# Attention outputs with the tile index innermost, turned and sent in later slots; other slots for the last attention steps; the residual in four double loads

## The chip, the core and the metric

The kernel runs on one core of one Trainium2 chip. The core has five engines that run side by side, each in its own program order, tied together by semaphores: PE (TensorE, matrix products), DVE (VectorE), ACT (ScalarE), POOL (GpSimd) and SP (SyncE, which here issues all transfers, in one queue, in program order). The metric is the time of one execution on the device in microseconds (us). Three executions of the kernel before took 1117.1, 1117.71 and 1118.11 us, the median being 1117.71 us.

## What is computed

One transformer block with its two branches side by side, for 2048 tokens of width 576, all in fp32:

```python
def _A_ref(x, wqkv, wo):             # H = 32 heads of 18, W = 8 keys, distance 2
    q, k, v = split(x @ wqkv)
    idx = pos[:, None] - 2 * arange(8)[None, :]      # 8 earlier tokens, masked below 0
    logits = einsum("bhsd,bhswd->bhsw", q, k[idx]) * scale
    attn = softmax(logits)
    o = einsum("bhsw,bhswd->bhsd", attn, v[idx])
    return o @ wo
def _B_ref(x, w1, b1, w2):           # 576 -> 4608 -> 576
    h = x @ w1 + b1
    return mish(h) @ w2
xn = layernorm(x)
return x + _A_ref(xn, wqkv, wo) + _B_ref(xn, w1, b1, w2)
```

## The kernel before

**Tiling.** The tokens are worked through in two halves of 1024, called `hf` 0 and 1. In a half, token p * 8 + j sits on partition p in tile j, so j (0 to 7, `TJ` = 8) is the tile index. Each fp32 operand of a product is split into a high part and a rest, and each product is the sum of three.

**Dense branch.** The 4608 hidden columns are taken 256 at a time, in 18 steps called quads (q = 0 to 17). A quad of a half is six parts of the first product (`m1_part`, 0 to 5, with Mish on ACT behind each finished bank and a rest for the second product on POOL, L719). The second product of quad q runs among the parts of quad q + 1; from quad 8 of half 1 on it comes in four chunks of 24 matrix instructions each (`m2_cols`, L878). Each chunk fills four PSUM banks, which DVE adds to the accumulators (L881). Four banks are all that this product has, so PE can run at most one chunk ahead of DVE.

**Attention.** It runs on POOL and DVE under the matrix work. The 32 heads of a half are taken four at a time, as eight pairs of units, and a pair takes nine steps: four in which POOL multiplies queries by shifted keys (L538), one with the softmax, four in which POOL multiplies the weights by shifted values (L576). DVE's sum over the product of a step (L543 into `L`, L582 into `og`) is issued at the start of the next step. After the fourth value sum of a pair, `o_send` is called at once: DVE turns `og` in 32x32 blocks into `oT` (L597), and SP sends `oT` with four transfers (L601) to `o_d`, a scratch tensor in the chip's memory. `og` has the layout [partition, tile, column], so the turn reads it with the tile index innermost, at steps of 72 elements.

**Output product.** At the end, `wo_part(p, part)` for p = 0 to 7 (two token tiles each, L1064) multiplies the attention outputs by `wo`. The outputs are loaded back by `o_load` (L890 and L893, three transfers a tile, into a ring of five buffers), summed and split by `o_split` (ACT L912 to L942, DVE L915 to L940, POOL L941 and L943), and DVE adds each finished bank to the residual (L1068). For half 0 the residual, x plus the dense branch, was put into the scratch tensor `y_d`; `y_load(j)` (L1039) fetches it tile by tile into the four-buffer ring `raw`, so the load of tile 4 waits until tile 0 has been sent to the output (L1074).

**Order.** It is written out by hand. `plan` is a list of slots, each a piece of PE work. Work of other engines is hung on slots with `before(slot, fn)`. In each slot there is run, in this order: what was put on the list `soon` during the slot before, the slot's hung work, and then PE's own work. At the end every engine's instructions are tied in program order. Attention steps are laid on slots by a table of rates and by the list `ok`, which says which slots of a quad may take one: for quads of half 1 from 10 on, slots 0, 3, 5, 7 and 9 of ten (slots 0, 1, 3, 5, 7 and 9 are parts of the first product there, 2, 4, 6 and 8 chunks; in quad 17, slots 3, 5, 7 and 9 are chunks). The last two steps of half 1 fall on the first two slots of the output product.

Of the kernel before, what the change touches and what calls it, by code (L numbers as in the profile page):

```python
# [8 lines left out]
F32 = mybir.dt.float32  # L9
# [8 lines left out]
P = 128  # L18
# [4 lines left out]
TJ = SH // P  # L23
# [16 lines left out]
def block_kernel(ctx: ExitStack, tc: tile.TileContext, x, wq, wo, w1, b1, w2, mask, out):  # L40
# [470 lines left out]
    def attention(hf):  # L511
        kqs = [load_kq(hf, k) for k in range(PU)]
        yield
        behind = [None]

        def flush():
            if behind[0] is not None:
                behind[0]()
                behind[0] = None

        for pair in range(NQ * UQ // PU):
            n = f"{hf}_{pair}"
            vs, nxt = [], []
            L = sb.tile([P, PU, TJ, W, 2], F32, tag="L", bufs=2, name=f"L_{n}")
            hj = TJ // 2
            for k, (kt, q) in enumerate(kqs):
                for c in range(2):
                    flush()
                    pr = sb.tile([P, hj, W, CU], F32, tag="pr", bufs=2, name=f"pr_{n}_{k}_{c}")
                    j0 = c * hj  # L530
                    hh = hj // 2
                    on = hf and pair == 0
                    if on:
                        nc.vector.tensor_tensor(
                            out=pr, in0=q[:, j0:j0 + hj, None, :].to_broadcast([P, hj, W, CU]),
                            in1=win(kt, 0, CU, j0, hj), op=ALU.mult)
                    for x in () if on else range(0, hj, hh):
                        nc.gpsimd.tensor_tensor(  # L538
                            out=pr[:, x:x + hh], in0=q[:, j0 + x:j0 + x + hh, None, :].to_broadcast([P, hh, W, CU]),
                            in1=win(kt, 0, CU, j0 + x, hh), op=ALU.mult)  # L540

                    def red(pr=pr, k=k, j0=j0, L=L):
                        nc.vector.tensor_reduce(  # L543
                            L[:, k, j0:j0 + hj].rearrange("p j w h -> p (j w h)"),
                            pr.rearrange("p j w (h d) -> p (j w h) d", h=2), axis=AX, op=ALU.add)
                    behind[0] = red
                    if k == 0:
                        vs.append(load_kv(hf, pair * PU + c, 1))
                    yield
            flush()  # L550
            if hf == 0:
                lm = L[0:2].rearrange("p k j w h -> p k (j w h)")
                nc.vector.tensor_add(lm, lm, mk[:, None, :].to_broadcast([2, PU, TJ * W * 2]))
            m = sb.tile([P, PU * TJ, 2], F32, tag="m", bufs=2, name=f"m_{n}")
            Lf = L.rearrange("p k j w h -> p (k j) w h")
            Lt = Lf.rearrange("p j w h -> p j h w")
            nc.vector.tensor_reduce(m, Lt, axis=AX, op=ALU.max)
            mb = m[:, :, None, :].to_broadcast([P, PU * TJ, W, 2])
            nc.vector.tensor_sub(Lf, Lf, mb)
            Ls = L.rearrange("p k j w h -> p (k j w h)")  # L560
            if (hf, pair) == (0, 4):
                soon.append(lambda: nc.scalar.preload_act_table_set("natural_log_exp_and_others"))
            soon.append(lambda Ls=Ls: nc.scalar.activation(Ls, Ls, AF.Exp, scale=SCALE))
            if (hf, pair) == (0, 4):
                soon.append(root1)
            yield
            nc.vector.tensor_reduce(m, Lt, axis=AX, op=ALU.add)
            nc.vector.reciprocal(m, m)
            nc.vector.tensor_mul(Lf, Lf, mb)  # L569
            og = sb.tile([P, TJ, PU * CU], F32, tag="og", bufs=1, name=f"og_{n}")  # L570
            for k, vt in enumerate(vs):
                for h in range(2):
                    flush()
                    pr = sb.tile([P, TJ, DH, W], F32, tag="pr", bufs=2, name=f"pv_{n}_{k}_{h}")
                    for x in range(0, TJ, hj):
                        nc.gpsimd.tensor_tensor(  # L576
                            out=pr[:, x:x + hj].rearrange("p j d w -> p j w d"),
                            in0=L[:, k, x:x + hj, :, h:h + 1].to_broadcast([P, hj, W, DH]),
                            in1=win(vt, h * DH, DH, x, hj), op=ALU.mult)

                    def red(pr=pr, og=og, c0=k * CU + h * DH, last=(k, h) == (PU - 1, 1), pair=pair):
                        nc.vector.tensor_reduce(og[:, :, c0:c0 + DH], pr, axis=AX, op=ALU.add)  # L582
                        if last:
                            o_send(hf, pair, og)
                    behind[0] = red
                    if (hf, pair, k, h) == (0, *(4, 0, 1)):
                        newton1()
                    if k == 0 and (pair + 1) * PU + h < NQ * UQ:
                        nxt.append(load_kq(hf, (pair + 1) * PU + h))
                    yield  # L590
            kqs = nxt
        flush()
        yield

    def o_send(hf, pair, og):
        oT = sb.tile([P, PU * CU * TJ], F32, tag="oT", bufs=1, name=f"oT_{hf}_{pair}")
        nc.vector.transpose(oT.rearrange("p (c j) -> p c j", j=TJ), og.rearrange("p j c -> p c j"))  # L597
        rows = o_d[hf][pair * PU * CU:(pair + 1) * PU * CU].rearrange("(n c) j p -> (c j) n p", c=4)
        for g in range(4):
            part = slice(g * 32, (g + 1) * 32)  # L600
# [433 lines left out]

    ys = {}

    def y_load(j):
        ys[j] = sb.tile([P, 5 * P], F32, tag="raw", bufs=4, name=f"y_{j}")
        nc.sync.dma_start(ys[j][:, 0:D], y_d.rearrange("(p j) d -> p j d", j=TJ)[:, j, :])  # L1039

    def y_store(j):
        nc.sync.dma_start(y_d.rearrange("(p j) d -> p j d", j=TJ)[:, j, :], accs[0][j])
# [3 lines left out]
    def wo_part(p, part):  # L1046
        hf, j = divmod(2 * p, TJ)
        od = ops[p]
        A, B, S = od["A"], od["B"], od["S"]
        ts = [ys[j + k][:, 0:D] for k in range(2)] if hf == 0 else None  # L1050
        ov = out[hf * SH:(hf + 1) * SH, :].rearrange("(p j) d -> p j d", j=TJ)
        A11, A12 = A[:, :, 0:2], A[:, :, 2:4]
        A22 = B[:, 0:2]
# [288 lines left out]
    def spot(hf, q, i):  # L1342
        return at["s", hf, q, i]
# [137 lines left out]
    for hf in range(NH):  # L1481
        for q in range(1, NP):
            for i in range(10):
                ok[spot(hf, q, i)] = i in ((0, 3, 7, 9), (0, 3, 5, 7, 9))[hf] and (q > 1 or i)

    for q in range(2 * OC + 2):
        for i in range(spot(1, q, 0), spot(1, q, 9) + 1):
# [42 lines left out]
    for n, name in enumerate(("T1", "T4", "D", "B22")):  # L1530
        before(j + n // 2, lambda name=name: wo_fetch(name))
    for k in range(2):
        before(j + -1, lambda k=k: (o_load(0, k), y_load(k)))
        before(at["o", 0, 0], lambda k=k: (o_load(0, 2 + k), y_load(2 + k)))
    for k in range(4):
        before(j + (1, 1, 2, 3)[k], lambda k=k: o_split(0, k, True))
    for k in range(4, 2 * TJ):
        before(at["o", k // 2 - 2, 0], lambda k=k: o_load(*divmod(k, TJ)))
        if k < TJ:
            before(at["o", k // 2 - 1, 1], lambda k=k: y_load(k))  # L1540

    for i, (fns, bg, _) in enumerate(plan):
        first, soon[:] = soon[:], []
# [49 lines left out]
```

## Time and profile before

| what | value |
|---|---|
| median of three executions | 1117.71 us |
| the profiled execution's own time | 1116.71 us |
| its span | 1114.9 us |
| PE busy | 1100.3 us, 99% of the span |
| DVE, POOL, ACT busy | 76%, 70%, 45% |
| granted TensorE clock | full in every slice |
| moved by DMA | 271.08 MB, mean 243 GB/s |

The span is the time from the first to the last instruction in the profile; the time of the profiled execution is 1.8 us longer, which lies around the span. A row of the timeline gives the start and the duration of a run of equal instructions, the engine, the line, the tiles as written<-read, and in square brackets the idle time of the engine before it and what ended it. "issue" there stands for time in which the engine waited for nothing that the profile shows. A row of the windows gives, for a stretch of time, the busy time of each engine with the number of instructions, the granted clock, the share of the DMA engines and the rate.

### The profile page before, as it was taken

Reading aid. Unit: us, or ns where it says so; the run is one execution under the profiler, and the core shown is the slowest. Engines: PE = TensorE matmul, PEld = TensorE weight load, DVE = VectorE, ACT = ScalarE, POOL = GpSimd, SP = SyncE. Lnnn points to the kernel's source line nnn. Section 1 sums busy time; section 2 is a strip of 40 time slices with the busy share of each in tenths; the row PEclk is TensorE's granted clock in tenths of the full one; section 3 lists DMA queues with packets and bytes.
Section 4 is the critical chain, followed back from the end, with each engine's and each line's share of the span. In section 5 each row is a group of like instructions: output and inputs, shape, how many; then the busy total and the mean of one; then the engine's idle time right before and its main releaser. Section 6 shows DMA issues by size and latency. Waiting matters only on the chain.

```text
span 1114.9 us, 18235 instructions
## 1 busy us (share of the span) xinstructions
PE 1100.3 (99%) x6550; PEld 1013.6 (91%) x6550; DVE 852.4 (76%) x1371; ACT 497.9 (45%) x916; POOL 776.8 (70%) x631
## 2 busy tenths in 40 slices
PE   8999999999999999999999999999999999999998
PEld 7999899999999999999999889988999999999898
DVE  6369788888889888897666576686776677787886
ACT  5544645544554534555232355353442443433353
POOL 2479777766679687785787336666779878768732
PEclk9999999999999999999999999999999999999999
DMA  6899696868766849666697797664665466876664
GB/s 205 282 312 317 221 351 215 293 226 276 263 242 240 295 152 365 236 240 216 189 336 251 215 368 263 234 220 145 240 219 186 173 231 220 291 239 198 220 202 140
DMA packets 175134, 271.08 MB, mean 243 GB/s; under 512 B 49570, under 2 KB 116420, under 8 KB 175044
## 3 DMA queue, kind: packets, MB, share of 16 engines
q1 hardware_dynamic: 175044, 269.91, 70.9%
q8 instruction: 52, 0.85, 0.3%
q14 instruction: 38, 0.31, 0.1%
HBM read 160.39 MB, written 109.48 MB: 242 GB/s over the span
## 4 chain that ended last, share of the span: by engine, by line
PE 87%; DVE 4%; POOL 3%; DMA 2%; ACT 1%; issue 1%; SPq 1%; DVEq 0%; ACTq 0%; POOLq 0%
PE h L667 29%; PE po L765 21%; PE pq L348 9%; PE po L878 9%; PE po L857 7%; PE h L673 6%; PE o L1064 4%; PE z L446 3%; DMA o<-o_d 1%; POOL pv L576 1%; POOL s L618 1%; DVE og L582 1%; POOL accP L866 1%; DMA wo<-wkept_B 1%; POOL act L719 0%
## 5 line engine op out<-in xcount | busy, mean ns | idle before, releaser
L765 PEld LDWEIGHTS po<-w,act 128*128 128x128 f32 x1728 | 236.4, 188 | 6.0 <-POOL act L719 0.4
L765 PE MATMUL po<-w,act 128*128 128x288 f32 x1728 | 240.7, 295 | 0.1
L576 POOL TENSOR_TENSOR pv<-L,kv 128x576 f32<-128x576 f32 x128 | 175.9, 1472 | 38.1 <-DVE L L569 28.6
L719 POOL TENSOR_TENSOR act<-c,act 128x512 fp32r<-128x512 f32 x81 | 107.7, 1330 | 126.2 <-ACT act L718 125.5
L538 POOL TENSOR_TENSOR pr<-q,kv 128x576 f32<-128x576 f32 x120 | 184.2, 1560 | 6.4 <-DMA q<-q_d 4.6
L769 DVE TENSOR_TENSOR acc<-po,acc 128x288 f32<-128x288 f32 x288 | 119.5, 448 | 29.6 <-PE po L765 28.3
L348 PE MATMUL pq<-wq,xt 128*128 128x432 f32 x672 | 136.3, 361 | 1.0 <-ACT xt L81 0.6
L878 PEld LDWEIGHTS po<-w,act 128*128 128x128 f32 x960 | 131.1, 188 | 4.3 <-DVE accP L881 1.0
L878 PE MATMUL po<-w,act 128*128 128x288 f32 x960 | 133.9, 295 | 0.6 <-DVE accP L881 0.5
L348 PEld LDWEIGHTS pq<-wq,xt 128*128 128x128 f32 x672 | 125.1, 188 | 7.8 <-ACT xt L81 1.4
L713 ACT ACTIVATE c<-c,b1c 128x512 f32<-128x512 f32 x81 | 58.7, 725 | 135.1 <-DVE c L712 134.7
L667 PE MATMUL h<-xt,t 128*128 128x512 f32 x432 | 110.5, 391 | 0.7 <-DVE rt L712 0.7
L667 PE MATMUL h<-S,t 128*128 128x512 f32 x432 | 110.4, 391 | 0.0
L582 DVE TENSOR_REDUCE og<-pv 128x144 f32<-128x1152 f32 x64 | 85.9, 1343 | 26.9 <-POOL pv L576 26.7
L701 ACT COPY c<-h 128x512 f32<-128x512 f32 x81 | 47.5, 586 | 129.7 <-PE h L673 75.3
L667 PE MATMUL h<-xt,wa 128*128 128x512 f32 x432 | 104.1, 390 | 0.0
L543 DVE TENSOR_REDUCE L<-pr 128x64 f32<-128x1152 f32 x64 | 85.8, 1342 | 15.0 <-POOL pr L538 14.9
L667 PEld LDWEIGHTS h<-xt,wa 128*128 128x128 f32 x432 | 80.9, 188 | 17.0
L881 DVE TENSOR_TENSOR accP<-po,accP 128x288 f32<-128x288 f32 x160 | 69.5, 453 | 34.4 <-PE po L878 33.1
L857 PEld LDWEIGHTS po<-pw,u 128*128 128x128 f32 x672 | 92.1, 188 | 2.9 <-DVE u L811 0.7
L857 PE MATMUL po<-pw,u 128*128 128x288 f32 x672 | 93.7, 295 | 0.5 <-DVE u L811 0.5
L667 PEld LDWEIGHTS h<-xt,t 128*128 128x128 f32 x432 | 79.0, 188 | 15.7 <-DVE rt L712 1.2
(229 smaller groups left out, 1850.8 us busy)
## 6 DMA issues: line engine op xcount, KB each, us to landing
kv<-kv_d SPq DMA_DIRECT2D x64, 396.0 KB, 5.3
kept_t<-t SPq DMA_DIRECT2D x36, 512.0 KB, 5.3
t<-kept_t SPq DMA_DIRECT2D x36, 512.0 KB, 5.5
rw<-in_w SPq DMA_DIRECT2D x36, 320.0 KB, 4.5
kept_wa<-wa SPq DMA_DIRECT2D x18, 640.0 KB, 5.5
kept_w<-w SPq DMA_DIRECT2D x20, 576.0 KB, 5.2
wa<-kept_wa SPq DMA_DIRECT2D x18, 640.0 KB, 5.0
w<-kept_w SPq DMA_DIRECT2D x20, 576.0 KB, 4.2
```

Of the source, the lines that this page charges most:

```text
L348: nc.tensor.matmul(pq[:, 0:432], XT[:, xi, tok], wt[wi][:, hl, 0:432], start=i == 0, stop=i == len(seq) - 1)
L538: nc.gpsimd.tensor_tensor(out=pr[:, x:x + hh], in0=q[:, j0 + x:j0 + x + hh, None, :].to_broadcast([P, hh, W, CU]), in1=win(kt, 0, CU, j0 + ...
L543: nc.vector.tensor_reduce(L[:, k, j0:j0 + hj].rearrange("p j w h -> p (j w h)"), pr.rearrange("p j w (h d) -> p (j w h) d", h=2), axis=AX, ...
L576: nc.gpsimd.tensor_tensor(out=pr[:, x:x + hj].rearrange("p j d w -> p j w d"), in0=L[:, k, x:x + hj, :, h:h + 1].to_broadcast([P, hj, W, DH]),
L582: nc.vector.tensor_reduce(og[:, :, c0:c0 + DH], pr, axis=AX, op=ALU.add)
L667: nc.tensor.matmul(ph, wt[:, wl, wk * P:(wk + 1) * P], X[:, xs, :], start=first and i == 0, stop=last and i == len(seq) - 1, skip_group_ch ...
L719: nc.gpsimd.tensor_tensor(out=a[:, 1, :], in0=t, in1=a[:, 0, :].bitcast(F32), op=ALU.subtract)
L765: nc.tensor.matmul(po, acts[hf, q, b, j][:, al, tok], done["w2", hf, 2 * q + j][:, wl, c * HC:(c + 1) * HC], start=i == 0, stop=i == 5)
L769: nc.vector.tensor_tensor(out=t, in0=po, in1=t, op=ALU.add)
L857: nc.tensor.matmul(po, units[e, k, qq][:, al, tok], w[:, qq, wl, :], start=i == 0, stop=i == 5)
L878: nc.tensor.matmul(po, acts[hf, q, b, j][:, al, tok], done["w2", hf, 2 * q + j][:, wl, c * HC:(c + 1) * HC], start=i == 0, stop=i == 5)
L881: nc.vector.tensor_tensor(out=t, in0=po, in1=t, op=ALU.add)
```

## The change

It has four parts.

1. `og` gets the layout [partition, column, tile]. The value sums (L582) now write it at steps of eight elements, and the turn reads it in one run.
2. After the last value sum of a pair, the turn (`o_turn`) is put on `soon`, so it is issued at the start of the next slot; the turn puts `o_send` on `soon` in its place, so the four transfers are issued at the start of the slot after that.
3. In the last four quads of half 1 (14 to 17), slot 1 may take an attention step too. From the fourth step of pair 5 (of 0 to 7) on, the steps move up along the allowed slots: by one place in quad 14, two in quad 15, three in quad 16 and four in quad 17. The last product moves from the first slot of the output product to the first of the four chunks of quad 17 ahead of it, the last sum to the second chunk; the last turn is in the third, the last send in the fourth.
4. The residual of half 0 is loaded two tiles at a time, four loads in place of eight, into the four-buffer ring `w2` (which held the weights of the second product) in place of `raw`. The four loads stand at one slot after the first of quad 17's own chunks, at the first and third slot of the output product's p = 0, and at the third of p = 1.

In the built program PE's order is the same instruction for instruction. ACT gets one more load of an activation table: the exponential of the last pair now stands ahead of the last Mish instructions and not behind them. In SP's queue the last `oT` now stands behind the first residual load and ahead of `o_load` of tiles 2 and 3; before, it stood behind tiles 2 to 5.

```diff
-            og = sb.tile([P, TJ, PU * CU], F32, tag="og", bufs=1, name=f"og_{n}")
+            og = sb.tile([P, PU * CU, TJ], F32, tag="og", bufs=1, name=f"og_{n}")
...
-                        nc.vector.tensor_reduce(og[:, :, c0:c0 + DH], pr, axis=AX, op=ALU.add)
+                        nc.vector.tensor_reduce(og[:, c0:c0 + DH, :].rearrange("p d j -> p j d"), pr, axis=AX,
+                                                op=ALU.add)
                         if last:
-                            o_send(hf, pair, og)
+                            soon.append(lambda: o_turn(hf, pair, og))
...
-    def o_send(hf, pair, og):
+    def o_turn(hf, pair, og):
         oT = sb.tile([P, PU * CU * TJ], F32, tag="oT", bufs=1, name=f"oT_{hf}_{pair}")
-        nc.vector.transpose(oT.rearrange("p (c j) -> p c j", j=TJ), og.rearrange("p j c -> p c j"))
+        nc.vector.transpose(oT, og.rearrange("p c j -> p (c j)"))
+        soon.append(lambda: o_send(hf, pair, oT))
+
+    def o_send(hf, pair, oT):
...
-    def y_load(j):
-        ys[j] = sb.tile([P, 5 * P], F32, tag="raw", bufs=4, name=f"y_{j}")
-        nc.sync.dma_start(ys[j][:, 0:D], y_d.rearrange("(p j) d -> p j d", j=TJ)[:, j, :])
+    def y_load(p):
+        ys[p] = sb.tile([P, 2, D], F32, tag="w2", bufs=4, name=f"y_{p}")
+        nc.sync.dma_start(ys[p], y_d.rearrange("(p j) d -> p j d", j=TJ)[:, 2 * p:2 * p + 2, :])
...
-        ts = [ys[j + k][:, 0:D] for k in range(2)] if hf == 0 else None
+        ts = [ys[p][:, k] for k in range(2)] if hf == 0 else None
...
-                ok[spot(hf, q, i)] = i in ((0, 3, 7, 9), (0, 3, 5, 7, 9))[hf] and (q > 1 or i)
+                ok[spot(hf, q, i)] = i in ((0, 3, 7, 9), (0, 3, 5, 7, 9))[hf] + (1,) * (hf and q >= NP - 4) and (q > 1 or i)
...
-        before(j + -1, lambda k=k: (o_load(0, k), y_load(k)))
-        before(at["o", 0, 0], lambda k=k: (o_load(0, 2 + k), y_load(2 + k)))
+        before(j + -1, lambda k=k: o_load(0, k))
+        before(at["o", 0, 0], lambda k=k: o_load(0, 2 + k))
...
+    for p_ in range(TJ // 2):
+        before((j + 1, at["o", 0, 0], at["o", 0, 2], at["o", 1, 2])[p_], lambda p_=p_: y_load(p_))
     for k in range(4, 2 * TJ):
         before(at["o", k // 2 - 2, 0], lambda k=k: o_load(*divmod(k, TJ)))
-        if k < TJ:
-            before(at["o", k // 2 - 1, 1], lambda k=k: y_load(k))
```

## The prediction

> **What bounds the kernel now.** I read the busy times first, then stretches, then the timeline of PE where a stretch has gaps.
>
> ```profile
> PE 1100.3 (99%) x6550; PEld 1013.6 (91%) x6550; DVE 852.4 (76%) x1371; ACT 497.9 (45%) x916; POOL 776.8 (70%) x631
> ```
> ```profile
> 1045.00:1055.00 10.00, 9.33 (x67) 8.65 (x65) 9.92 (x21) 3.67 (x9) 10.00 (x9) 1.00 0.46 126
> 1055.00:1065.00 10.00, 7.14 (x52) 6.93 (x53) 8.96 (x18) 3.31 (x9) 4.24 (x4) 1.00 0.29 66
> ...
> 1075.00:1085.00 10.00, 8.97 (x68) 8.73 (x67) 7.43 (x18) 4.95 (x12) 3.38 (x3) 1.00 0.70 213
> 1085.00:1095.00 10.00, 10.00 (x76) 9.89 (x76) 8.35 (x22) 5.76 (x15) 4.38 (x4) 1.00 0.64 203
> ```
>
> PE is the bound, so only its gaps can be won. In each row the stretch's length is followed by PE, PEld, DVE, ACT and POOL. PE has gaps where the last attention steps lie in the output product (DVE 99% and 90% busy) and once more near 1079. From 1085 on PE is full although DVE is at 84%. The timeline of PE gives the sizes:
>
> ```profile
> 1046.10 6.89 PE L878 MATMUL po<-w,act 128*128 128x288 f32 x48 [0.51 <-DVE accP L881]
> 1052.83 1.76 PE L1064 MATMUL o<-wo,oa 128*128 128x288 f32 x12
> ...
> 1055.87 1.86 PE L1064 MATMUL o<-wo,oS 128*128 128x288 f32 x12 [1.02 <-DVE y L1068]
> 1059.98 1.03 PE L1064 MATMUL o<-wo,oS 128*128 128x288 f32 x6 [1.99 <-issue]
> 1062.97 1.75 PE L1064 MATMUL o<-wo,oa 128*128 128x288 f32 x12
> 1079.64 1.86 PE L1064 MATMUL o<-wo,oS 128*128 128x288 f32 x12 [1.03 <-DVE y L1068]
> 1084.55 1.76 PE L1064 MATMUL o<-wo,oa 128*128 128x288 f32 x12
> 1111.22 0.43 PE L1064 MATMUL o<-wo_r,ob 128*128 128x288 f32 x2
> ```
>
> A row on `oa` starts each p. p = 4 to 7 take 1111.65 - 1084.55 = 27.1 us, 6.78 each. p = 0 takes 1062.97 - 1052.83 = 10.14. Who held PE shows on DVE and SP:
>
> ```profile
> 1056.96 1.34 DVE L582 TENSOR_REDUCE og<-pv 128x144 f32<-128x1152 f32 x1
> 1058.34 1.21 DVE L597 STREAM_TRANSPOSE oT<-og 128x576 f32<-128x576 f32 x1
> 1059.47 0.78 DVE L1068 TENSOR_TENSOR y<-o,y 128x288 f32<-128x288 f32 x2
> ```
> ```profile
> 1038.83 0.42 SPq L890 DMA_DIRECT2D o<-o_d  x1
> ...
> 1048.20 1.15 SPq L893 DMA_DIRECT2D o<-o_d  x2
> 1059.57 1.99 SPq L601 DMA_DIRECT2D o_d<-oT  x4
> ...
> 1067.94 1.06 SPq L1039 DMA_DIRECT2D y<-y_d  x2
> ...
> 1075.90 1.06 SPq L1039 DMA_DIRECT2D y<-y_d  x2
> ```
> ```profile
> 1075.90 3.13 DMA y<-y_d
> ```
>
> The add at 1059.47 comes behind the last sum and the last turn, and PE goes on at 1059.98: the "issue" gap is DVE's. The gap at 1079 is the residual of p = 3, issued only at 1075.90 (its ring's buffer was free late, and SP had stood 10 us at the last `oT`); the chain of waits runs through its landing.
>
> **The change, part by part.**
>
> *Last steps out of the output product.* All eight p together take 1111.65 - 1052.83 = 58.8 us. Eight at 6.78 would take 54.2. So 4.6 us can go: 3.4 in p = 0, 1.2 in p = 1 to 3, most of that the residual. Two sums (1.34 each) and the turn leave DVE there; what is late next comes below. Term: -4.6.
>
> *The residual in `w2`.* Its four buffers hold all eight tiles, so no load waits for an output. The first needs quad 16's last chunk, the third and fourth quad 17's; all are issued at least one p ahead of their use. The landings need a few us, and 6.78 lie between. Half as many issues leave SP. This is in the term above; if a load were late again, 1.0 comes back.
>
> *Work pushed into the four quads.* What ran after 1038.85 must now run earlier:
>
> ```profile
> 1038.85:1060.00 21.15, 5.38 (x4) 9.72 (x8) 1.00 0.52 167
> ...
> sum 144.57, PE 144.57 PEld 132.37 DVE 109.17 ACT 57.35 POOL 108.96; mean PE 24.09 PEld 22.06 DVE 18.20 ACT 9.56 POOL 18.16
> 1021.70 5.60 POOL L538 TENSOR_TENSOR pr<-q,kv 128x576 f32<-128x576 f32 x4
> 1013.41 4.91 POOL L576 TENSOR_TENSOR pv<-L,kv 128x576 f32<-128x576 f32 x4
> 1039.44 1.31 POOL L719 TENSOR_TENSOR act<-mn,act 128x512 fp32r<-128x512 f32 x1 [1.88 <-ACT act L718]
> ```
>
> The first row is the value products and sums after 1038.85 (DVE, then POOL), the second the mean over six stretches of one quad each, 894 to 1039. Spread over four quads, the moved work adds 9.72 / 4 = 2.4 us of POOL and, with a score sum and the softmax of pair 7, some 2.2 of DVE. POOL comes to 20.6 of 24.1, DVE to 20.4. Both fit; PE pays only where a chunk's four banks wait longer than the part between two chunks covers. I followed slots with a product step of 2.8 (row 1021.70, half) or 2.5 (row 1013.41) and L719 at 1.3. In quads 14 to 16 the sum is always done while banks are still free. Quad 17 has the tight place: its steps in slots 9, 0 and 1 put two score products and L719 in a row on POOL, and the last sum, the softmax's front and then the evictions of the first chunk come about 0.1 late at 1.40 an instruction. At 1.53 (row 990.25 below) it is 0.9. Ends 0 and 1.2; I take 0.4, since row 1021.70 is from this very quad.
>
> *The chunks of quad 17.* POOL's last product cannot start before L719 at 1039.44 ends (1040.75), so it ends at 1043.2 and the last sum on DVE at 1044.6.
>
> ```profile
> 1044.28 0.41 DVE L915 TENSOR_TENSOR s<-ot,o 128x256 f32<-128x256 f32 x1
> ...
> 1045.60 1.54 DVE L881 TENSOR_TENSOR accP<-po,accP 128x288 f32<-128x288 f32 x4
> ```
>
> The softmax that stood ahead of L915 is gone, yet L915 starts at 1044.6 against 1044.28, and the evictions at 1045.9 against 1045.60. The gap of 0.51 grows to some 0.8, and the turn one chunk later takes the place of a sum of equal length; with its 1.3 us another 0.25. Together +0.5 (ends 0 and 1.0).
>
> *The send ahead of tiles 2 and 3.* This is a new wait. The turn ends at about 1048.7 (evictions 1045.9 + 1.54, turn 1.3). SP then issues four sends (1.99, row 1059.57) and behind them tile 2, which before was out at 1038.83, at 1050.8, and tile 3 at 1052.4 (0.4 and 1.2 us each, rows 1038.83 and 1048.20). `o_split` of p = 1 reads tile 3 first, on ACT, and DVE's L915 waits for it with the adds of p = 0 queued behind. How long a load takes depends on the traffic; the two rows are the landings of L890 in 1025 to 1036 and in 1064 to 1069:
>
> ```profile
> DMA to landing us min/median/max: 8.2/8.2/8.2
> ...
> DMA to landing us min/median/max: 2.8/2.8/2.8
> ```
>
> With 2.8 tile 3 is there at 1055.2 to 1056, ACT's copy and L915 with L918 pass by 1057, and the add that PE needs at 1056.8 is 0.1 to 0.9 late. With 8.2 it is 5.4 late. The stretch from 1055 to 1065 moved 66 GB/s, so I take the short landing: +0.4, ends 0 and 5.4. Tiles 4 to 7 come in time at 6.78 a p.
>
> *The turn's layout.* Between these rows lies its price:
>
> ```profile
> L597 DVE STREAM_TRANSPOSE oT<-og 128x576 f32<-128x576 f32 x16 | 21.1, 1322 | 0.5
> ...
> L799 DVE TENSOR_TENSOR rm<-ra,rm 128x512 f32<-128x512 f32 x6 | 4.1, 680 | 0.8 <-ACT rm L713 0.8
> ```
>
> Read in one run, 576 elements at the pace of the second row (clear of its slow neighbours) would take about 0.77; the other end is 1.32 unchanged. I take 0.8, being nearer to a contiguous read. It matters where DVE holds PE: in the third chunk above, ahead of tiles 2 and 3, and at
>
> ```profile
> 777.56 1.33 DVE oT L597
> ...
> 780.07 0.61 DVE rt L712
> 780.73 1.67 PE h L667 x6
> ```
>
> where the turn is in the chain ahead of an add that PE waits for: up to 0.55. Term: -0.4 (ends 0 and -1.1). The Trainium skill (SBUF — State Buffer, section Door 1: The DMA port swizzle) says that SBUF has lines of 16 bytes and an access that crosses to a new one pays. The old read, 288 bytes a step, fits the 1322 ns; by the rule alone the turn shortens, as I took it. But the rule speaks against the sum, which now writes at 32 bytes a step: by it 144 writes would pay. Of that no row shows a case; a sum writes once in eight reads, and L582's 1.34 is that of the read, so I take 0, at most 0.15 a sum if each write cost one cycle more, and that lies beside PE nearly everywhere.
>
> *The rest.* Turns and sends one slot later in the other pairs: their reader is the output product, and PE is full there; the loads now ahead of them in SP's queue leave earlier. If that cover fails, a weight load is late by at most the 2.0 of a send. The extra table load
>
> ```profile
> 1039.38 1.28 ACT L563 ACT_TABLE_LOAD   x1
> ```
>
> falls on ACT, 9.56 of 24.1 busy in these quads; between the copies that free PE's banks it has a chunk of room. 0; without that cover 1.3.
>
> **Sum.** -4.6 + 0.4 + 0.5 + 0.4 - 0.4 = -3.7 us against the profiled execution's 1116.71 (span 1114.9): 1113.0. The median shown, 1117.71, is 1.0 above that execution, so I predict 1114.0 for the median.
>
> **Rivals.**
>
> *Tiles 2 and 3 land late (no change).* If the loads behind the send take 5 us instead of 2.8, PE waits 2.2 more and the gain is 1.5: 1116.2. For it: seven and eight us a few slots earlier, and more transfers now lie close together. Against it: the low rate of that stretch.
>
> *POOL and DVE crowd each other (slower).* The place is quads 14 to 17.
>
> ```profile
> 990.25 6.13 POOL L538 TENSOR_TENSOR pr<-q,kv 128x576 f32<-128x576 f32 x4
> ```
>
> This pair of steps took 6.13, not 5.60. At 0.3 more a step, for the 5.3 product steps of a quad, POOL needs 22.2 of 24.1 us, sums come behind their slots and hold the evictions. If PE loses 1.7 us a quad, 6.8 in all instead of 0.4, the kernel is slower by 2.7: median 1120.4. From 1.6 a quad on it decides by over 0.2%. Against it: PE has no gap in these quads with POOL at 18.2, and four banks give slack. The Trainium skill (GPSIMD Engine Reference, Specifications) says POOL shares its SBUF interfaces with DVE and contends with DVE instructions that have two SBUF inputs; no run here has yet separated that, but 1.40 against 1.53 fits.
>
> *The output product does not speed up.* If DVE with the adds alone held PE, only the residual's 1.0 would come, less the 0.9 of the quads and chunks: about 1117.6. p = 4 to 7, without a gap, speak against it.
>
> **How the numbers follow.** A measurement tells this kernel from no change from about 0.2% on, 2.2 us. Forecast (-2.3 to -5.5): 0.65. Late tiles or no speed-up, within 2.2: 0.20. Crowding, slower: 0.14. More than -5.5, with the gaps outside the tail: 0.01. Faster 0.66, same 0.20, slower 0.14. The range runs from 1112.0, the forecast's gains at their best ends, to 1117.2, which takes in the late tiles; the likeliest case alone spans 1112.2 to 1115.4.
>
> **What would show it.** Right: p = 0 near 7 us, no L582 or L597 behind the first L1068, no residual load in the chain of waits, the turn near 0.8. Wrong: gaps on PE in 942 to 1039 ended by L881, tile 3 landing behind 1057, or p = 0 still near 10 us. What would make the prediction wrong is above all a chunk held by DVE in quad 17, where two steps stand in neighbouring slots.

## The result, and the profile after

The kernel before took 1117.71 us (median of 13 runs on the chip that timed both), the changed one 1115.18 us (13 runs): a ratio of 0.9978, 95% interval 0.997 to 0.9987. It is faster by 2.5 us, where 3.7 were forecast. One thing must be known to read the numbers: in some runs of ten of the fourteen kernels here TensorE ran at half its clock for some 3.4 us, which lengthens a run of the changed kernel by about 1.6 us and shows as a mean clock of 0.998. The profiled execution of the changed kernel (1116.75 us, span 1115.0) is such a run, that of the kernel before (1116.71, span 1114.9) is not. So the two spans look equal although the medians are not; 9 of the 13 runs of the changed kernel had the full clock, and their median is 1115.04.

The stretches that the prediction began with, in the changed kernel (behind the length come PE, PEld, DVE, ACT and POOL, and the granted clock is the third number from the right):

```profile
1045.00:1055.00 10.00, 9.05 (x69) 8.82 (x68) 9.04 (x21) 2.00 (x4) 2.61 (x2) 1.00 0.40 88
1055.00:1065.00 10.00, 7.99 (x49) 7.79 (x49) 5.58 (x14) 3.92 (x11) 1.45 (x2) 0.83 0.78 223
...
1075.00:1085.00 10.00, 10.00 (x77) 9.93 (x76) 8.31 (x21) 4.95 (x12) 3.24 (x3) 1.00 0.61 182
```

DVE is out of the way from 1055 on (5.58 of 10 where it had 8.96), and the stretch at 1075 is full (10.00, it had 8.97). The second stretch still has a gap of PE, and a clock of 0.83.

These are rows of PE in the timeline of the changed kernel that begin with one of the longer gaps, and the starts of the first five p of the output product. Code behind the turn stands four lines lower than before: L882 here is L878 there, L1068 is L1064.

```profile
783.32 3.21 PE L861 MATMUL po<-pw,u 128*128 128x288 f32 x22 [0.81 <-DVE u L815]
...
1026.92 3.45 PE L882 MATMUL po<-w,act 128*128 128x288 f32 x24 [0.46 <-DVE accP L885]
...
1047.69 6.63 PE L882 MATMUL po<-w,act 128*128 128x288 f32 x48 [0.95 <-DVE accP L885]
1054.16 1.76 PE L1068 MATMUL o<-wo,oa 128*128 128x288 f32 x12
...
1060.04 1.31 PE L1068 MATMUL o<-wo,oS 128*128 128x288 f32 x6 [2.01 <-ACT ot L932]
...
1064.56 1.75 PE L1068 MATMUL o<-wo,oa 128*128 128x288 f32 x12
1071.23 1.75 PE L1068 MATMUL o<-wo,oa 128*128 128x288 f32 x12
1077.94 1.75 PE L1068 MATMUL o<-wo,oa 128*128 128x288 f32 x12
1084.71 1.76 PE L1068 MATMUL o<-wo,oa 128*128 128x288 f32 x12
```

The gaps of 1.02 and 1.03 in p = 0 and p = 3 are gone, and no p behind the first takes over 6.8 us (1077.94 - 1071.23 = 6.71, 1084.71 - 1077.94 = 6.77). But the gap in the middle of p = 0 is as long as it was, 2.01 against 1.99, with another cause: it now ends when ACT has copied `ot`, not when DVE has turned `og`. Three gaps are new or longer: 0.81 at 782, 0.46 at 1026, 0.95 against 0.51 at 1046.

What ACT waited for stands in its own timeline, and the loads in SP's:

```profile
1058.40 0.38 ACT L916 COPY ot<-o 128x256 f32<-128x256 f32 x1 [5.78 <-DMA o<-o_d]
```
```profile
1049.44 1.98 SPq L605 DMA_DIRECT2D o_d<-oT  x4
1051.46 0.52 SPq L894 DMA_DIRECT2D o<-o_d  x1
...
1053.41 0.57 SPq L894 DMA_DIRECT2D o<-o_d  x1
```

Tile 3 is the last row. It was issued at 1053.41 behind the four sends and tile 2, and ACT could copy it at 1058.40, 5.0 us later; the view of DMA issues for 1048 to 1064 has the loads of L894 in that stretch at a median of 4.9 us, and gives the rate in 40 slices of 0.4 us:

```profile
GB/s 0 0 0 0 0 25 139 133 132 128 134 56 148 285 282 79 99 259 298 105 6 5 10 17 59 95 219 161 184 346 339 338 337 342 316 282 265 219 282 369
...
o<-o_d SPq DMA_DIRECT2D x4, 256.0 KB, 4.9
```

Where the clock was low, narrower stretches of the same execution show:

```profile
1054.00:1060.00 6.00, 4.03 (x31) 3.79 (x29) 2.57 (x8) 1.56 (x5) 0.00 (x1) 1.00 0.52 129
1060.00:1064.00 4.00, 3.96 (x18) 3.99 (x19) 2.72 (x7) 1.48 (x4) 1.27 (x1) 0.57 1.07 309
```

A mean of 0.57 over 4 us is 3.4 us at one half and 0.6 at full speed. It starts some 0.6 us behind the end of the gap of 2.01. What p = 0 would take without both is 1064.56 - 1054.16 = 10.40 less 2.01, less the 1.7 that 3.4 us at half clock cost: 6.7.

### The profile page after: what moved, and what is told of

It reads as the page before. It is cut to its first block, busy times and chain, and to the rows that moved or that the text cites. A ratio compares the mean times of both kernels' runs of the same rounds, so it can differ in the third digit from the quotient of the medians.

```text
span 1115.0 us, 18242 instructions
## 1 busy us (share of the span) xinstructions
PE 1102.7 (99%) x6550; PEld 1015.9 (91%) x6550; DVE 846.0 (76%) x1371; ACT 499.2 (45%) x917; POOL 777.4 (70%) x631
## 4 chain that ended last, share of the span: by engine, by line
PE 87%; POOL 6%; DVE 3%; issue 1%; ACT 1%; DMA 1%; SPq 1%; POOLq 0%; DVEq 0%; ACTq 0%
PE h L671 28%; PE po L769 21%; PE pq L348 9%; PE po L882 9%; PE po L861 7%; PE h L677 5%; PE o L1068 5%; PE z L446 3%; POOL pv L576 2%; POOL act L723 1%; POOL pr L538 1%; POOL s L622 1%; DVE u L815 1%; POOL accP L870 1%; PE ta L75 0%
## 5 line engine op out<-in xcount | busy, mean ns | idle before, releaser
L882 PEld LDWEIGHTS po<-w,act 128*128 128x128 f32 x960 | 130.9, 188 | 5.2 <-DVE accP L885 2.1
L882 PE MATMUL po<-w,act 128*128 128x288 f32 x960 | 133.6, 295 | 1.5 <-DVE accP L885 1.4
L582 DVE TENSOR_REDUCE og<-pv 128x144 f32<-128x1152 f32 x64 | 86.1, 1346 | 29.8 <-POOL pv L576 29.8
L543 DVE TENSOR_REDUCE L<-pr 128x64 f32<-128x1152 f32 x64 | 85.8, 1343 | 23.1 <-POOL pr L538 23.0
L705 ACT COPY c<-h 128x512 f32<-128x512 f32 x81 | 47.5, 586 | 119.2 <-PE h L677 65.8
L671 PEld LDWEIGHTS h<-S,t 128*128 128x128 f32 x432 | 77.9, 188 | 12.8
```

Of the source, the lines that this page charges most:

```text
L543: nc.vector.tensor_reduce(L[:, k, j0:j0 + hj].rearrange("p j w h -> p (j w h)"), pr.rearrange("p j w (h d) -> p (j w h) d", h=2), axis=AX, ...
L582: nc.vector.tensor_reduce(og[:, c0:c0 + DH, :].rearrange("p d j -> p j d"), pr, axis=AX, op=ALU.add)
L671: nc.tensor.matmul(ph, wt[:, wl, wk * P:(wk + 1) * P], X[:, xs, :], start=first and i == 0, stop=last and i == len(seq) - 1, skip_group_ch ...
L882: nc.tensor.matmul(po, acts[hf, q, b, j][:, al, tok], done["w2", hf, 2 * q + j][:, wl, c * HC:(c + 1) * HC], start=i == 0, stop=i == 5)
```

## The experiments

The theory: the last attention steps and the late residual cost what the sum says, and what is missing of the 3.7 us is tile 3, issued behind the last send. The rivals: a part of the change costs time by itself; the four quads are crowded. Each kernel was timed beside the kernel before on the same chip; "full-clock runs" are those with a mean clock above 0.998.

**The parts alone.** Part 4 (residual in `w2`) alone in the kernel before:

```diff
+        ys[p] = sb.tile([P, 2, D], F32, tag="w2", bufs=4, name=f"y_{p}")
```

> The kernel before with the residual in four double loads and nothing else. Theory (the late residual load held p = 3): the gap of 1.03 us near 1079 closes, 0.9 to 1.2 us faster than before, p = 1 to 3 together near 20.2 us instead of 21.6. Rival (the load was only the last of several waits there): the gap stays near 1 us with another releaser, and the time within 0.3 us of before.

It took 1116.72 us, ratio 0.9986 (0.9977 to 0.9994). In its timeline the gap of 1.03 ahead of 1079.64 is gone, those at 1055 (1.04) and 1058 (1.99) stay:

```profile
1055.98 1.86 PE L1064 MATMUL o<-wo,oS 128*128 128x288 f32 x12 [1.04 <-DVE y L1068]
...
1060.09 1.03 PE L1064 MATMUL o<-wo,oS 128*128 128x288 f32 x6 [1.99 <-issue]
...
1079.83 1.85 PE L1064 MATMUL o<-wo,oS 128*128 128x288 f32 x12
```

Part 4 is worth what p = 1 to 3 were to gain: by full-clock runs 1.4 us (1115.57, four runs, against 1116.93). Part 3 alone (slot 1 in quads 14 to 17):

```diff
+                ok[...] = i in (...)[hf] + (1,) * (hf and q >= NP - 4) and (q > 1 or i)
```

> The kernel before with slot 1 opened in the last four quads and nothing else: turn and send stay right behind the last sum. Theory: p = 0 comes down to about 7 us (3 us won), but the turn of 1.3 us now stands with the last sum ahead of the evictions of a chunk in quad 17, so PE's gap there is about 2 us instead of 0.5, and with 0.5 us near 1026 the net is 0.5 to 1.5 us faster than before; tiles 2 and 3 are not late, since the send leaves some 2 us earlier than in the changed kernel. Rival (crowding in quads 14 to 17): gaps on PE between 940 and 1040 sum to over 2 us and the kernel is no faster than before.

1117.54 us, ratio 0.9994 (0.9985 to 1.0003): no gain that can be measured, where 0.5 to 1.5 us were expected. Both gaps of p = 0 went, but a gap of 2.29 came ahead of the chunks, since turn and sum now stand there in a row, and the residual of p = 2 is late:

```profile
1048.99 8.17 PE L878 MATMUL po<-w,act 128*128 128x288 f32 x48 [2.29 <-DVE accP L881]
...
1073.33 1.85 PE L1064 MATMUL o<-wo,oS 128*128 128x288 f32 x12 [0.93 <-DVE y L1068]
```
```profile
1044.61 1.35 DVE L582 TENSOR_REDUCE og<-pv 128x144 f32<-128x1152 f32 x1 [0.60 <-POOL pv L576]
1046.00 1.27 DVE L597 STREAM_TRANSPOSE oT<-og 128x576 f32<-128x576 f32 x1
```

Moving the steps only moves the wait, from the output product into quad 17, unless the turn leaves the same slot. Part 1 alone (the layout of `og`):

```diff
+            og = sb.tile([P, PU * CU, TJ], F32, tag="og", bufs=1, name=f"og_{n}")
```

> The kernel before with the new layout of og and nothing else. Theory (the shorter turn is worth little because DVE then meets POOL at the shared access to SBUF): the turn takes 0.78 us, the gap of 0.7 near 780 closes and one of about 0.8 opens behind an instruction of DVE with two SBUF inputs that stretches from 0.7 to 1.8, p = 0 gets about 0.5 us shorter, net 0 to 0.7 us faster. Rival (every turn that DVE makes PE wait for pays in full): 1.0 to 1.5 us faster. The sums stay at 1.34.

1116.88 us, ratio 0.9986 (0.9977 to 0.9994). The turn takes 0.78 as in the changed kernel. But its full-clock runs, which are all 11, are no faster than the full-clock runs of the kernel before on that chip (1116.88 against 1116.93). What the ratio shows is that none of them fell to half clock, where 19 of 33 of the kernel before did; the gap at 1058 is down from 1.99 to 1.56. Part 2 alone (turn and send put off by a slot each):

```diff
-                            o_send(hf, pair, og)
+                            soon.append(lambda: o_turn(hf, pair, og))
```

> The kernel before with the turn one slot and the send two slots later, and nothing else. Theory (hidden): no gap on PE goes or comes before 1040, and in the output product the last turn only moves by a part, within 0.6 us of before. Rival (the loads that leave earlier because SP no longer stands at the turn matter): over 0.6 us faster, with a gap of before gone between 560 and 830.

1119.83 us, ratio 1.0021 (1.0012 to 1.003): slower, which was not expected. SP's queue shows why: the last send comes later, behind a store that waits for DVE, and with it all that stands behind it. The residual of p = 2 (L1042) is issued at 1070.20, and PE waits 2.30 us for the add that needs it:

```profile
1062.73 1.63 SPq L1077 DMA_DIRECT2D out<-y  x2
1064.41 2.15 SPq L604 DMA_DIRECT2D o_d<-oT  x4
...
1070.20 1.06 SPq L1042 DMA_DIRECT2D y<-y_d  x2
```
```profile
1073.95 1.86 PE L1067 MATMUL o<-wo,oS 128*128 128x288 f32 x12 [2.30 <-DVE y L1071]
```

By full-clock runs the four parts alone are worth -0.05, +1.9, -0.45 and -1.4 us, which adds up to nothing (of part 2 only two runs had the full clock, of part 4 four). Together they are worth some -2.0: 1115.04 against 1117.0, the median of the 44 full-clock runs of the kernel before beside the experiments, since the clocks of its 13 runs beside the changed kernel are not on record. The gain comes of the combination.

**The missing gain.** The changed kernel with tiles 2 and 3 loaded ahead of the last send:

```diff
-        before(at["o", 0, 0], lambda k=k: o_load(0, 2 + k))
+        before(j + 2, lambda k=k: o_load(0, 2 + k))
```

> The changed kernel with the loads of tiles 2 and 3 issued ahead of the last send (at the third of quad 17's own chunks) and nothing else. Theory (these loads behind the send cost the 2.0 us in p = 0): the wait for tile 3 goes, p = 0 comes down to about 7 us, 1.5 to 2.2 us faster than the changed kernel. Rival (DVE or POOL holds the same place anyway): the gap in p = 0 stays over 1 us with another releaser, under 0.5 us won.

1113.05 us (1112.78 to 1113.69), ratio 0.9957 (0.9944 to 0.9971), 2 us below the changed kernel. SP has both tiles out before the send, and PE goes through p = 0 in 1060.53 - 1053.89 = 6.64 us:

```profile
1041.91 0.58 SPq L894 DMA_DIRECT2D o<-o_d  x1
...
1049.18 1.99 SPq L605 DMA_DIRECT2D o_d<-oT  x4
```
```profile
1047.43 6.62 PE L882 MATMUL po<-w,act 128*128 128x288 f32 x48 [0.94 <-DVE accP L885]
1053.89 1.75 PE L1068 MATMUL o<-wo,oa 128*128 128x288 f32 x12
...
1057.59 0.96 PE L1068 MATMUL o<-wo,oS 128*128 128x288 f32 x6
...
1060.53 1.75 PE L1068 MATMUL o<-wo,oa 128*128 128x288 f32 x12
```

The theory holds for the size and the place of this wait. On top of that kernel, turn and send in the slot of the last sum again:

> The changed kernel with tiles 2 and 3 ahead of the last send, and turn and send in the slot of the last sum again, as in the kernel before. Theory (putting the turn and send off costs time alone, 1.0021, because it moves the send in front of late loads; with the other parts the last sum lies in quad 17's own chunks and nothing that is late stands behind the send, so only the place of the turn counts): the last turn, 0.78, now stands on DVE ahead of a chunk's four evictions, the gap of 0.94 at that chunk grows to 1.3 to 1.7, and the kernel takes 0.3 to 0.8 us more than with the turn put off: ratio 0.9961 to 0.9964. Rival (putting off costs time by itself in the other seven pairs too): the kernel is faster without it, ratio 0.994 to 0.9955.

1114.74 us, ratio 0.9974 (0.9965 to 0.9983), 1.7 more than with the turn put off, where 0.3 to 0.8 were expected. The gap ahead of the chunks is 1.74, just above what was expected. But the test isn't pure: the send moves ahead too (1046.80), tiles 2 and 3 stand behind it again (L890 at 1050.58 and 1052.45), and 0.73 of the loss is a wait for tile 3. So putting the turn off, which costs 1.9 alone, saves time here: 0.8 of the 1.7 is the longer gap ahead of the chunks (1.74 against 0.94), because the turn stands again in the chunk that the last sum already holds.

The changed kernel with the old layout of `og`:

> The changed kernel with the old layout of og: the turn takes 1.33 us again. Theory (the shorter turn is nearly given back near 783): the gap near 783 behind the stretched DVE instruction goes and the one of 0.7 near 780 is back, which is 0.2 to 0.3 better there; the send and tile 3 come 0.5 later, and p = 0 loses that: 0 to 0.7 us slower than the changed kernel. Rival (the turn pays in full everywhere): 1.0 to 1.5 us slower.

1116.11 us, ratio 0.9986 (0.9977 to 0.9995), where the changed kernel had 0.9978: in company the layout is worth some 0.9 us of the medians, 0.3 of full-clock runs (1.75 below the kernel before on that chip, against the 2.0 above), and the intervals overlap. Its trace shows where the turn's gain went. DVE and POOL at 780 in the changed kernel:

```profile
780.01 1.54 DVE L867 TENSOR_TENSOR accP<-po,accP 128x288 f32<-128x288 f32 x4
781.47 1.80 DVE L815 TENSOR_TENSOR u<-rm,u 128x512 fp32r<-128x512 f32 x1
```
```profile
781.44 1.28 POOL L815 TENSOR_TENSOR u<-rm,u 128x512 fp32r<-128x512 f32 x1 [3.96 <-ACT u L809]
```

and with the old layout:

```profile
781.25 1.54 DVE L866 TENSOR_TENSOR accP<-po,accP 128x288 f32<-128x288 f32 x4
782.71 0.68 DVE L814 TENSOR_TENSOR u<-rm,u 128x512 fp32r<-128x512 f32 x1
```
```profile
782.68 1.87 POOL L814 TENSOR_TENSOR u<-rm,u 128x512 fp32r<-128x512 f32 x1 [4.52 <-ACT u L808]
```

In both the two engines do the same operation on the two halves of `u`, and POOL starts 0.03 us ahead. With the old layout POOL is the slower one (1.87) and DVE takes 0.68; with the new one POOL takes 1.28 and DVE 1.80, and PE, which needs DVE's half, waits 0.81. What decides which of them loses was not tried; the 0.03 us by which POOL is ahead is the same in both.

**The four quads.** The changed kernel with slot 1 open in five quads, 13 to 17, and the same with tiles 2 and 3 first:

```diff
-... (1,) * (hf and q >= NP - 4) ...
+... (1,) * (hf and q >= NP - 5) ...
```

> The changed kernel with slot 1 opened in the last five quads instead of four, so that every step from quad 14 on comes one place earlier and the last product stands ahead of the last chunk rest on POOL. Theory: the gap of 0.95 us in quad 17 falls to 0.5 or less, and the send leaves a chunk (3 us) earlier, so that the wait for tile 3 goes too: 2 to 3 us faster than the changed kernel, with up to 0.5 us of new gaps in quads 13 to 17. Rival (crowding): the gaps from 915 to 1040 grow by over 1.5 us and less than 1 us is won.

> Both of the two edits before. Theory: what the five quads leave of the wait for tile 3 goes, 2 to 3 us faster than the changed kernel, within 0.5 us of the five quads alone. Rival (the loads ahead of the send meet the fetch of the output weights): slower than the five quads alone by over 0.5 us.

1119.47 us, ratio 1.0016 (1.0007 to 1.0025), and 1117.07 us, 0.9988 (0.998 to 0.9997). Tiles first is worth 2.4 us here as well; without it PE still waits 1.77 for tile 3, which the earlier send was to end. Both have a gap of 2.48 at 1026, and are slower than the changed kernel where 2 to 3 us faster was expected. ACT with five quads:

```profile
1025.27 0.73 ACT L717 ACTIVATE c<-c,b1c 128x512 f32<-128x512 f32 x1 [5.88 <-DVE c L716]
...
1026.67 1.28 ACT L563 ACT_TABLE_LOAD   x1
1027.96 0.42 ACT L563 ACTIVATE L<-L 128x256 f32<-128x256 f32 x1
1028.29 0.57 ACT L705 COPY c<-h 128x512 f32<-128x512 f32 x1
```
```profile
1028.90 2.00 PE L671 MATMUL h<-S,t 128*128 128x512 f32 x6 [2.48 <-ACT c L705]
```

The copy of `h`, which frees the bank that PE needs, stands behind the table load and the exponential of the last pair, 1.70 us together. Ahead of these ACT had stood 5.88 us until DVE's L716, which came at 1024.56 behind the last score sum (1022.37) and the front of the softmax. Two kernels were to tell this from crowding in quad 17's first slots, both with tiles first: slot 1 open in quads 13 to 16, and in 12 to 16.

> The changed kernel with tiles 2 and 3 ahead of the last send, and slot 1 opened in quads 13 to 16 in place of 14 to 17. All four score sums of pair 7 but the last then come one open slot earlier, and slot 1 of quad 17 is free of a step, while the steps of quad 17's slot 3 and later stay where they were. Theory (the gap of 0.46 us ahead of quad 17's first chunk is crowding: a score sum and the front of the softmax ahead of the evictions): that gap falls to 0 to 0.2, nothing else moves, and the kernel takes 0.3 to 0.5 us less than with slots 14 to 17, a ratio to the kernel before of 0.9953. Rival (the crowding only moves to quad 13, where the run with five open quads had a gap of 0.38 near 956): a gap of 0.3 to 0.5 shows in 930 to 960 and the ratio stays at 0.9957 or goes to 0.996.

> The changed kernel with tiles 2 and 3 ahead of the last send, and slot 1 opened in quads 12 to 16. The softmax of pair 7 then falls in quad 17's first slot, one step earlier than with quads 14 to 17, and the last product in its last slot but one. Theory (five open quads lost 2.5 us at 1026 because table load and exponential stood on ACT ahead of a copy that frees a bank for PE): here too they stand ahead of the copies of quad 17's second part, so a gap near 2.5 stays at 1026, the gap at 1046 falls to 0.3 as with five quads, and the ratio is that of tiles_first_five, 0.998 to 0.9995. Rival (the gap came from the two steps in slots 0 and 1 of quad 17, which are not both taken here): the gap falls below 1 us and the kernel is as fast as with 14 to 17 or faster, 0.995 to 0.996.

13 to 16: 1113.85 us, ratio 0.9967 (0.9955 to 0.9979). The gap at 1026 is gone, so it was the step in quad 17's slot 1; a gap of 0.38 came at 955, again ahead of a copy on ACT that stands behind an exponential (`<-ACT c L705`). That is what the rival had said. The time is 0.8 above tiles first, more than the gaps account for. The starts of the same rows in the two timelines show where it goes: the row `h<-S,t` at 950 comes 0.2 later than with tiles first (950.62 against 950.42), the row `h<-xt,t` at 961 1.4 later (961.37 against 960.00), the chunks at 1047 0.8 later (1048.19 against 1047.43). So the crowding around that copy costs 1.2 us, of which the bracket shows 0.38, and the gap that is gone at 1026 gives half of it back. 12 to 16: 1112.9 us, ratio 0.9963 (0.995 to 0.9975), as fast as tiles first. There I had expected the gap of 2.5, and it is not there; the rival had said so: it put the gap down to the two steps in slots 0 and 1 of quad 17. On ACT the exponential stands ahead of the copy as with five quads, but the softmax is done sooner:

```profile
1020.34 0.42 ACT L563 ACTIVATE L<-L 128x256 f32<-128x256 f32 x1 [0.57 <-DVE L L559]
1020.77 1.28 ACT L717 ACT_TABLE_LOAD   x1
...
1023.35 0.58 ACT L705 COPY c<-h 128x512 f32<-128x512 f32 x1
```

So it isn't the place in ACT's queue alone that costs. With five quads two steps in a row make DVE's L716 late, and the table load and the exponential come on top of that when the copy is due; with the exponential 7.6 us earlier, and L716 at 1020.22, the copy is on time. The gap at 1046 falls to 0.33, one of 0.60 comes at 912.

**The half clock.** A look through all runs set against the longest gap of PE behind the start:

| kernel | longest gap, us | runs at 0.998 or less |
|---|---|---|
| tiles first; 12 to 16; 13 to 16 | 0.94; 0.79; 0.99 | 0 of 16 |
| layout alone | 1.56 | 0 of 11 |
| no putting off | 1.74 | 2 of 10 |
| before (beside the experiments) | 1.99 | 46 of 90 |
| residual alone; changed | 1.99; 2.01 | 7 of 11; 4 of 13 |
| old layout; slots alone | 2.13; 2.29 | 4 of 11; 6 of 11 |
| putting off alone; five quads; five, tiles first | 2.30; 2.48; 2.48 | 9 of 11; 10 of 11; 7 of 11 |

That reads as if a long gap lets the clock fall. To try it, tiles first with the very last sum done twice, which lengthens a gap and changes no result:

```diff
+                        if last and n0 == "1_7":
+                            nc.vector.tensor_reduce(og[:, c0:c0 + DH, :].rearrange("p d j -> p j d"), pr, axis=AX,
+                                                    op=ALU.add)
```

> The changed kernel with tiles 2 and 3 ahead of the last send (no gap of PE over 1 us in the second half of the kernel, and none of its 5 runs with a mean clock below 1.000), with the very last sum of the attention done twice. It adds 1.35 us on DVE ahead of the four evictions that PE waits for at 1046, so the gap of 0.94 becomes 2.2 to 2.4. Theory (a gap of about 2 us lets TensorE's clock fall to half for some 3.4 us in a part of the runs): the undisturbed runs take 1.35 us more, 1114.4, and a part of the runs, 3 in 10 to 9 in 10, show a clock of 0.998 and take some 1.5 us more than that, near 1116. Rival (the half clock has nothing to do with the gap, but with the stage or the chip): all runs keep a clock of 1.000 and take 1114.4.

1114.96 us, ratio 0.9981 (0.9972 to 0.999). 5 of 11 runs had a mean clock of 0.998 or less and took 1115.74 to 1117.93; the six others took 1114.69 to 1114.96. The gap is 2.41, and the profiled execution has the half clock around its end:

```profile
1049.71 7.97 PE L885 MATMUL po<-w,act 128*128 128x288 f32 x48 [2.41 <-DVE accP L888]
```
```profile
1040.00:1048.00 8.00, 7.30 (x56) 7.07 (x54) 6.50 (x10) 2.20 (x6) 3.85 (x3) 1.00 1.05 376
1048.00:1054.00 6.00, 4.29 (x22) 4.30 (x23) 5.10 (x13) 1.38 (x3) 1.28 (x1) 0.72 0.30 50
```

0.72 over 6 us is again 3.4 us at one half. The 48 matmuls took 7.97 instead of 6.62. Against 0 of 5 runs of tiles first, 5 of 11 alone would be thin. But in each of the seven profiled executions with a mean clock of 0.998 (changed, residual alone, slots alone, old layout, five quads, five with tiles first, sum twice) the clock behind the start is below 1.00 in one place only, and that is at its longest gap, wherever this lies: the half clock begins between 0.5 us before the gap's end and 1.1 us behind it and lasts 3.4 us. The long gap is shown as the cause; why only a part of the runs fall is open.

## Why the prediction was right, and where not

The direction, and the time within the range, were right: 1115.18 against 1114.0, in 1112.0 to 1117.2. Part of the nearness is luck. The forecast left the half clock out; the changed kernel fell to it in 4 of 13 runs, the kernel before in 46 of 90, which adds some 0.5 to the gain of the medians. By full-clock runs the gain is 2.0. By its steps:

*Last steps out of the output product, -4.6.* Right, but only where tile 3 doesn't wait. p = 1 to 3 took 1084.71 - 1064.56 = 20.15 us against 21.58, 1.4 less where 1.2 were forecast. p = 0 took 6.64 with tiles first, where the sum had 6.78. In the changed kernel itself the wait for tile 3 took 2.0 of the 3.4 that p = 0 was to gain.

*Tiles 2 and 3 behind the send, +0.4.* The term that was mis-sized most: it measured 2.0. The chain was there, and the rival "late tiles" had named it: with 5 us for the load PE waits 2.2 more. The load left at 1053.41 and not at 1052.4, and took 4.9 to 5.0 where the sum had 2.8. Why it took so long is open. The rate does not explain it: the stretch of the row with 2.8, 1064 to 1069 before, moved 214 GB/s, while the rate was 119 GB/s from issue to copy here, and next to nothing from 1056.0 to 1057.6, as the slices above show. So a low rate was no ground for the short landing. The time measured lies between the likeliest case's 1114.0 and that rival's 1116.2.

The other terms are best read from the starts of PE's rows. The idle time in brackets is counted from the modelled end of the matmul before, so it can be too small.

*The turn, -0.4.* The turn itself came out as taken:

```profile
L598 DVE STREAM_TRANSPOSE oT<-og 128x576 f32<-128x576 f32 x16 | 12.4, 775 | 0.4
L582 DVE TENSOR_REDUCE og<-pv 128x144 f32<-128x1152 f32 x64 | 86.1, 1346 | 29.8 <-POOL pv L576 29.8
```

775 ns instead of 1322. By the rule of the Trainium skill (SBUF — State Buffer, section Door 1: The DMA port swizzle) a read within a line is cheaper than one that crosses, and the trace agrees for the read. For the write, where the same rule spoke against the sum, it does not show: the 64 sums write at 32 bytes a step and take 1346 ns, against 1343 before. At 780 the gap fell from 0.72 to 0.17, the 0.55 that the sum had as its end, and some 0.55 was gained at 595, where the turn also stood in PE's chain. But next to it lies the new gap of 0.81 at 782, where DVE now meets POOL, and it costs 1.1 in the starts:

```profile
785.85 1.53 PE L667 MATMUL h<-S,wc 128*128 128x512 f32 x6
```
```profile
780.15 1.65 PE L671 MATMUL h<-xt,t 128*128 128x512 f32 x6 [0.17 <-DVE rt L716]
...
786.37 1.54 PE L671 MATMUL h<-S,wc 128*128 128x512 f32 x6
```

The first row is of the kernel before, where 5.12 us lie between it and 780.73; in the changed kernel it is 6.22. Counted from the row `tb<-ident,xn` at 556, which drops what differs at the start, the row `h<-S,wc` at 786 comes after this many us:

| kernel | old layout | new layout |
|---|---|---|
| turn in the slot of the last sum | 229.88 (before) | 229.86 (layout alone) |
| turn in the same slot, tiles first | | 229.88 |
| turn and send put off | 230.25 (putting off alone), 230.28 (changed, old layout) | 230.30 (changed) |

The changed kernel and the six that differ from it only behind 786 lie within 230.18 to 230.30. So up to here the faster turn is worth nothing. The Trainium skill's sentence on POOL (GPSIMD Engine Reference, Specifications) that it contends with DVE instructions of two SBUF inputs fits the pair at 781, 0.68 against 1.80, though no run here keeps the two apart.

*The rest, 0.* Wrong: putting turn and send off costs 0.4 us in the pairs before 786, as the same table shows, with either layout. Part of it, 0.2, lies at 731, where a run of L857's matmuls starts later (731.08 with putting off alone, 730.85 before); what holds it there is open.

*Crowding, +0.4.* Right in place, somewhat larger: the gap of 0.46 at quad 17's first chunk puts the rows behind it 0.7 later (from 0.6 behind the kernel before at 1025.85 to 1.3 at 1032.05), and quads 14 to 16 have none. It is the step in quad 17's slot 1, as the run without it shows.

*The chunks of quad 17, +0.5.* Right in place, but it cost nothing in the end. The gap grew by 0.95 - 0.51 = 0.44, but the rows around it make that up: PE is 1.33 behind the kernel before at 1032.05 (there 1030.72) and 1.33 behind at the first row of the output product (1054.16 against 1052.83). The further 0.25 in the third chunk did not come.

*The extra table load, 0.* Right in the changed kernel. That its cover is a matter of time is shown by five quads, where load and exponential took 1.70 of ACT's time just ahead of a copy for which PE waited 2.48; the sum had 1.3 as the price without cover, and left out the exponential.

*The median 1.0 above the profiled execution.* The prediction carried this 1.0 along without a cause. Some 0.7 of it is the half clock: the kernel before fell to it in 46 of 90 runs, and its other runs have a median of 1117.0. The changed kernel's gap is as long but stands alone, where before one of 1.03 came 3 us ahead of it; it fell in 4 of 13. Whether the pair of gaps makes the difference was not tried.

Added up, the output product begins 1.3 later than before, p = 0 takes 1.4 less once the half clock's 1.7 is taken off (8.7 against 10.14), and p = 1 to 3 take 1.4 less: -1.5 between the two profiled executions, where the sum had -3.7. Late tiles (1.6 more than forecast) and the 0.8 of turn and putting off make most of the difference; the chunks, which cost nothing, go the other way.

Of the rivals, late tiles is what happened to PE; the crowding of POOL and DVE in quads 14 to 17 did not come, and the output product did speed up.

## What to carry to other kernels

When work is moved ahead in a queue, price the loads that now stand behind it with all the landings that the trace has and not with the shortest (2.8, 4.9 and 8.2 us here for the same load, and the rate around it did not tell the 2.8 from the 4.9), and look first whether they can be put ahead of it: here one line was worth 2 us, as much as the whole change. A wait that is taken from one stage is given to another unless each piece of the chain (sum, turn, send) gets its own slot: slots alone brought nothing, putting off alone cost 1.9 us by full-clock runs, both together paid. Read what a gap costs from the starts of the rows behind it and not from its idle time alone: 0.81 idle cost 1.1 here. And count the gaps of TensorE by length: a longest gap of 1.74 us or more cost in part of the runs another 1.6 us of half clock, one of 1.56 or less in none, so that one long gap is worse than several short ones.

## What the runs showed of the hardware that was not expected

A gap of TensorE of 2 to 2.5 us lets its clock fall to half for some 3.4 us in 4 of 13 to 10 of 11 runs of a kernel, one of 1.74 us in 2 of 10; with gaps of up to 1.56 us no run did so (0 of 27). The Trainium skill (TensorE: Matmul & The Clock Gate, section Part 1: The HAM clock gate) describes a monitor with free-running windows of about 3.4 us and a half clock after an idle one. The length of the stretch, 3.4 us in the seven profiled executions that have one, agrees. The bound does not: gaps of 1.74 to 2.48 us were enough, in a part of the runs.

A turn of 128x576 fp32 took 1.32 us when it read at 288 bytes a step and 0.78 when it read in one run, while a reduction that began to write at 32 bytes a step kept its 1.34. And a DVE operation of 512 elements took 0.68 or 1.80 us beside the same operation on POOL (1.87 or 1.28), by which of the two had the upper hand. The load of one tile's 256 KB took 2.8, 4.9 or 8.2 us to land.
